# One score pass instead of two for the last head of each group, in a fused attention and feed-forward kernel

## The chip, the cores and the metric

The kernel runs on one core of one Trainium2 chip. A core has a matrix engine (TensorE, in the profile PE, its weight loads PEld), a vector engine (DVE), a scalar engine for activations (ACT), a general one (POOL) and a queue engine that issues transfers (SP). The metric is device time in microseconds. Before the change the median of three runs is 551.24 us (550.49 to 552.46).

## The reference

The input x has 2048 rows of 448. Two branches are computed from it and mixed by a gate per row. Branch A is attention with a memory, in 4 segments of 512 rows and 16 heads of 28; branch B is a feed-forward layer of width 1792.

```python
for s in range(N):                                 # N = 4 segments, L = 512 rows
    qs, ks, vs = q[:, :, s], k[:, :, s], v[:, :, s]
    logits = jnp.einsum("bhqd,bhkd->bhqk", qs, ks) * scale + mask   # causal: -1e9 above
    p = _softmax(logits, axis=-1)
    a_dot = jnp.einsum("bhqk,bhkd->bhqd", p, vs)
    ...                                            # a_mem from the memory M, z of earlier segments
    outs.append(g * a_mem + (1.0 - g) * a_dot)
    ...
o = ... @ wo
b = _silu(x @ w1) @ w2
gate = _sigmoid((x * gate_w).sum(-1, keepdims=True))
return gate * o + (1 - gate) * b
```

The weights of q and k are 200 times their usual size, so the logits are large and each row's maximum has to be taken off before the exponential.

## The kernel before

float32 values are carried as pairs of float16 halves (a high part and a remainder), so most products are three matmuls that add into one bank. The work is in three stages.

1. `project`: scales of all inputs, the projections to q, k and v, the memory of the segments. q, k and v go to buffers in device memory in the layouts that the later stages read.
2. Attention, 16 groups `t` (4 segments by 4 groups) of 4 heads, together with pass 1 of the feed-forward layer (10 of its 14 blocks of 128, for all 4 segments).
3. Pass 2 of the feed-forward layer (the other 4 blocks), the output product with `wo`, and the mix. The second products of pass 2 may not start until every group's attention is stored (`attended`). The first products of pass 2 may.

Each group reads its q and k into one buffer, `ring`. Then each head goes through two score passes:

- In `maxima`, queries lie on partitions. A 512-row segment gives four row blocks i of 128 queries with 128(i+1) keys, 1280 score columns a head. DVE adds the causal mask and takes the row maximum (line 744; for the first blocks of all four heads together, line 739, with the mask added by a matmul, line 730). The maxima are transposed, split into halves and sent through device memory into two extra rows of `ring` (`mscr`, lines 752 to 759).
- In `attention`, the scores are computed again with keys on partitions and those two extra rows, so that the maximum is already taken off (line 1328, 86 rows deep, again 1280 columns). ACT takes the exponential in three pieces (line 1333). POOL sets the parts above the diagonal to zero (lines 1336 and 1339), ACT makes the high half of all 1280 columns (line 1345) and POOL the remainder in three pieces (line 1349). Keys on partitions is the layout that the product with the values needs (line 1362): 20 matmuls a head, 10 blocks for each half.

DVE adds up the result (line 1370). After four heads the group is divided by its sums and stored (`o_scr`).

The order of all instructions on every engine is fixed when the kernel is built: `Sched` is a list scheduler with a cost for each operation. Each engine takes what can start first and, among those, what has the smallest `prio`. Head n of the 64 has `prio` 10 n, its product with the values `PVP` later, the remainder `LOP` later; the feed-forward pass spreads from `FLO` to `FHI` over the same scale. On the chip each engine then runs its list in that order, waiting on semaphores. Buffers are rings; a ring with no free buffer makes the taker wait. The score banks are the three of `BK["sc"]`. The feed-forward halves are in a ring of `NW` = 12 buffers (`ghl`).

Transfers with a transpose are there before only for the output product: `features` (line 654) turns a 128 by 896 float16 tile into seven 128 by 128 blocks, on SP's queue.

Of the kernel before, what the change touches and what calls it, by code (L numbers as in the profile page):

```python
# [19 lines left out]
NG = 4  # L20
# [10 lines left out]
NEG = -1.0e30  # L31
# [6 lines left out]
HPRIO = 26.57  # L38
# [4 lines left out]
NW = 12  # L43
# [4 lines left out]
WOT = 258.31  # L48
# [3 lines left out]
LOP = 66.17  # L52
LATE = -0.07
FIRST = 104.6
WPRIO = 91.56
MAXO = 57.4
# [3 lines left out]
MP = 23.61  # L60
VF = -52.52
VA = 12.88
VS = 2.68
NV = 8
XH0 = -44.21
NF = 4
VE = 10.92
LASTQ = 6.3
WQS = -136.22
VH = 44.78  # L70
XS0 = -76.47
VC = -7.5
OT1 = -114.26
XS = 34.75
QS = -34.17
KS1 = -32.16
SS = -9.2
# [6 lines left out]
PRICE = 235.91  # L84
PRICE2 = 67.41
SLACK2 = 0.33
PVRUNS = [((1, 0), 1)]
PVP = 79.52
FLO = 50.28
FHI = 729.09  # L90
WOP = 8.33
SZ = 16.64
SZSTEP = 1.72
XPRIO = 345.51
WBP = 34.36
# [183 lines left out]
def infini_mix(ctx: ExitStack, tc: tile.TileContext, x, wq, wk, wv, wo, beta, w1, w2, out):  # L279
# [120 lines left out]
    es = const.tile([128, NSEG + 1], F32, name="es")  # L400
    wide = const.tile([128, 2 * NSEG], F32, name="wide")
# [123 lines left out]
    def by(o, i, a, b=None, op0=OP.mult, op1=OP.mult):  # L525
        if b is None:
            nc.gpsimd.tensor_scalar(o, i, a, None, op0=op0)
        else:
            nc.gpsimd.tensor_scalar(o, i, a, b, op0=op0, op1=op1)  # L529
# [20 lines left out]
    def others(s, prio, bds, own, t_own, t_gh):  # L550

        def mem():
            z = spk[:, NSEG + s:NSEG + s + 1]
            by(z, top[:, WK:WK + 1], top[:, xi(s)], 1.0 / FIT)
            by(z, z, 1.0 / UP, op0=OP.max)
            by(bds[:, s, :, DH:], own[:, :, None], z[:GW])
            by(bds[:, s, :, :DH], own[:, :, None].to_broadcast([GW, 4, DH]), z[:GW], rv[:GW, s:s + 1])

        def go():
            by(rv[:, s:s + 1], top[:, WV:WV + 1], top[:, xi(s)], 1.0 / FIT)  # L560
            by(omgs[:, s], omg, rv[:, s:s + 1])
# [12 lines left out]
        EREADY[s] = few(5, scores, PREADY[s], SCALED[WQ], SCALED[WK], prio=prio + 0.5)  # L574
        END1.append(EREADY[s])
# [134 lines left out]
    def maxima(t, o):  # L710
# [11 lines left out]
        plan = [(0, [0, 1, 2, 3]), (1, [0, 1]), (1, [2, 3])] + [(i, [h]) for h in range(4) for i in (2, 3)]  # L722
        for q, (i, hs) in enumerate(plan):
            ps = Buf(BK["sc"])
            n = 128 * (i + 1)
            p0 = o - MAXO + 40 * q / len(plan)

            def go(i=i, hs=hs, ps=ps, n=n):
                if i == 0:
                    nc.tensor.matmul(ps.v, identb, maskb[:, None, :].to_broadcast([128, 4, 128]), start=True,  # L730
                                     stop=False, skip_group_check=True)
                for j, hh in enumerate(hs):
                    u = j * n
                    nc.tensor.matmul(ps.v[:, u:u + n], rg.v[:KS, 0, hh, i * 128:(i + 1) * 128], rg.v[:KS, 1, hh, :n],  # L734
                                     start=(i > 0), stop=(i > 0 or j == 3), skip_group_check=(i == 0))

            def red(i=i, hs=hs, ps=ps, n=n):
                if i == 0:
                    nc.vector.tensor_reduce(mx.v[:, :, 0], ps.v.rearrange("p (h n) -> p h n", h=4), axis=AX.X,
                                            op=OP.max)  # L740
                    return
                for j, hh in enumerate(hs):
                    r = ps.v[:, j * n:(j + 1) * n]
                    nc.vector.tensor_tensor_reduce(r, r, MK[:, L - n:], 1.0, NEG, OP.add, OP.max,  # L744
                                                   mx.v[:, hh, i:i + 1])
            m = pe((half(512) if i == 0 else []) + half(n, len(hs)), go, *rs, *MKS, takes=[ps], uses=[rg], prio=p0)
            reds.append(dve(len(hs) * (n + 184) if i else 512, red, m, *reds[:1], takes=[] if reds else [mx], uses=[ps, mx],
                            prio=p0))
# [3 lines left out]
        f1 = pe(half(128), lambda: nc.tensor.transpose(pt.v[:16, :128], mx.v.rearrange("p h i -> p (h i)"), ident), *reds,  # L752
                takes=[pt], uses=[mx], prio=p0)
        f3 = act(128, lambda: nc.scalar.activation(mh.v[:, 0], pt.v[:16, :128], AF.Copy, scale=1.0 / TALL), f1, takes=[mh],
                 uses=[pt], prio=p0)
        f4 = dve(128, lambda: nc.vector.scalar_tensor_tensor(mh.v[:, 1], pt.v[:16, :128], 1.0 / TALL, mh.v[:, 0],
                                                             op0=OP.mult, op1=OP.subtract), f3, uses=[pt, mh], prio=p0)
        d1 = dma(16e3, lambda: start(mscr[t].rearrange("z h i n -> (h i) z n"), mh.v), f4, uses=[mh], prio=p0)
        dm = dma(16e3, lambda: start(rg.v[KS:KS + 2, 0], mscr[t].rearrange("z h i n -> z h (i n)")), d1, uses=[rg],
# [427 lines left out]
    TH, GF, PA = (tiles(fp, n, [128, L], F32, 2) for n in ("th", "gf", "pa"))  # L1187
# [66 lines left out]
    def spare(s, p0, m):  # L1254
        th, gf, g = Buf(TH), Buf(GF), Buf(GTR)
        if s not in SP:
            fetch_spare(s, p0)
        h, e0 = SP[s]
        e1 = copy(L + 110, lambda: nc.scalar.activation(th.v, h.v, AF.Tanh, scale=wide[:, NSEG + s:NSEG + s + 1]), e0, m,
                  takes=[th], uses=[h], prio=p0)  # L1260
        e2 = dve(L, lambda: nc.vector.scalar_tensor_tensor(gf.v, th.v, 1.0, h.v, op0=OP.add, op1=OP.mult), e1,
                 port=True, takes=[gf], uses=[h, th], prio=p0)
        e3 = copy(L + 110, lambda: nc.scalar.activation(g.v[:, 0], gf.v, AF.Copy, scale=hso[:, s:s + 1]), e2, m, takes=[g],
                  uses=[gf], prio=p0)
        e4 = scaled(L, lambda e: rest(e, g.v[:, 1], gf.v, hso[:, s:s + 1], g.v[:, 0]), e3, uses=[gf, g], prio=p0)
        return g, [e3, e4]

    def part(s, tb, ps, lasts, prio):
        k = s * TB + tb
        a = Buf(PA)  # L1270
        w = act(D + 110, lambda: nc.scalar.activation(a.v[:, :D], ps.v[:, :D], AF.Copy, scale=ogs[:, k:k + 1]),
                lasts[-1][0], takes=[a], uses=[ps], prio=prio)
        PST[k] = dma(229e3, lambda: start(pscr[s][tb * 128:(tb + 1) * 128, :], a.v[:, :D]), w, uses=[a], prio=prio)
# [25 lines left out]
    cring("phl", [128, 2, 1280], F16, 3, cp)  # L1299
    cring("oraw", [128, 4, TB, DH + 1], F32, 2, cp)  # L1300
# [3 lines left out]
    t_one = [ONE[1]] + [ones_rows(i) for i in range(1, 4)]  # L1304

    def attention(t):
# [9 lines left out]
        for hh in range(4):  # L1316
            n = 4 * t + hh
            p0 = 10.0 * n
            pf, hl = Buf(C["pf"]), Buf(C["phl"])
            ex, mk = [], []  # L1320
            for b in range(3):
# [14 lines left out]
            mk.append(pool(80, lambda pf=pf: nc.gpsimd.affine_select(  # L1336
                pf.v[:, 1, 384:], pf.v[:, 1, 384:], [[1, 128]], OP.is_ge, 0.0, base=0, channel_multiplier=-1), ex[1],
                uses=[pf], prio=p0))
            mk.append(pool(204, lambda pf=pf: nc.gpsimd.affine_select(  # L1339
                pf.v[:, :, :128], pf.v[:, :, :128], [[0, 3], [1, 128]], OP.is_ge, 0.0, base=0, channel_multiplier=-1),  # L1340
                *ex, uses=[pf], prio=p0))
# [6 lines left out]
            for u, w in zip((0,) + CUTS, CUTS + (1280,)):  # L1348
                low = pool(w - u + 22, lambda hl=hl, flat=flat, u=u, w=w: nc.gpsimd.tensor_sub(  # L1349
                    hl.v[:, 1, u:w], flat()[:, u:w], hl.v[:, 0, u:w]), low, uses=[pf, hl], prio=p0 + LOP,  # L1350
                    lat=0.0 if w < 1280 else LATE)
            ps = Buf(BK["cc"])
            last = None
            for zs, ready in PVRUNS:
                def go(zs=zs, ps=ps, hl=hl, hh=hh):
# [9 lines left out]
                last = pe([m for z in zs for m in [(max(x, 0.027), y) for x, y in half((58, 29)[z], 10)]], go, dv, (hi, low)[ready], last,  # L1365
                          takes=[ps] if last is None else [], uses=[ps, hl, vg], prio=p0 + PVP)

# [3 lines left out]
            fins.append(dve(232, fin, last, *fins[:1], takes=[] if fins else [orw], uses=[ps, orw], prio=p0 + PVP))  # L1371
# [146 lines left out]
```

## Time and profile before

| | |
|---|---|
| median of 3 runs | 551.24 us |
| profiled execution, its own time | 550.28 us |
| its span (first to last instruction) | 548.5 us |
| time around the span | 1.8 us |
| PE busy | 539.2 us (98%) |
| ACT busy | 409.0 us (75%) |
| DVE busy | 401.5 us (73%) |
| POOL busy | 354.3 us (65%) |
| DMA engines, mean busy share | about 50% |

A busy time is the union of an engine's instructions; a PE that counts as busy need not be at its peak, since matmuls overlap. The profile also gives: busy time in chosen stretches of the span; the chain of work that ended last, followed back from the last instruction, with the start and the length of each piece; groups of instructions, with the busy time, the mean length of one, the idle time of the engine just before them and what ended it; the instructions in order of time; and the waits.

### The profile page before, as it was taken

The numbers are of one execution on the slowest core, as the hardware profiler recorded it, in microseconds if no ns is written. First come the engines' busy times: TensorE is split into PE (matmuls) and PEld (weight loads), VectorE is DVE, ScalarE is ACT, GpSimd is POOL, SyncE is SP. The second block draws the span as 40 slices with busy tenths as digits, with TensorE's granted clock in tenths as the row PEclk, the third lists the DMA queues.
The fourth block names the chain that finished last, engine by engine and source line by source line (L and its number), as shares of the span: only waits on it lengthen the run. The fifth ranks groups of instructions, "written<-read, shape, count | busy, mean of one in ns | idle before, by whom it ended". The sixth has DMA issues, their size and how long they took to land.

```text
span 548.5 us, 11583 instructions
## 1 busy us (share of the span) xinstructions
PE 539.2 (98%) x4044; PEld 299.7 (55%) x4044; DVE 401.5 (73%) x989; ACT 409.0 (75%) x700; POOL 354.3 (65%) x546
## 2 busy tenths in 40 slices
PE   8999999999999999999999999999999999999997
PEld 3445656556644556555565555565555555555544
DVE  5998989898668985598555788757886239754482
ACT  5978899677359978999787998889997897501140
POOL 3345374686406788899888898898998986112120
PEclk9999999999999999999999999999999999999999
DMA  8777867544467343324233234546211211689963
GB/s 300 254 238 225 243 180 219 166 148 131 140 190 189 95 129 92 103 71 120 55 112 93 70 97 115 152 121 175 56 36 36 87 54 50 238 226 233 241 177 99
DMA packets 78059, 78.94 MB, mean 144 GB/s; under 512 B 44168, under 2 KB 67720, under 8 KB 78000
## 3 DMA queue, kind: packets, MB, share of 16 engines
q1 hardware_dynamic: 77424, 77.21, 48.8%
q10 hardware_dynamic: 576, 0.99, 0.6%
q8 instruction: 32, 0.52, 0.4%
q14 instruction: 27, 0.22, 0.1%
HBM read 48.41 MB, written 26.09 MB: 136 GB/s over the span
## 4 chain that ended last, share of the span: by engine, by line
PE 74%; ACT 7%; DVE 7%; POOL 6%; DMA 3%; issue 2%; SPq 0%; DVEq 0%; ACTq 0%; POOLq 0%
PE mm L629 19%; PE mm L1232 17%; PE sc L629 8%; PE sc L1328 6%; PE sc L734 5%; PE cc L1362 5%; PE cc L1232 5%; PE cc L629 5%; ACT pf L1333 3%; DMA rawf<-in_w_dram 2%; PE sc L989 2%; POOL es L529 1%; ACT phl L1345 1%; DVE stg L931 1%; DMA raw<-in_wv_dram 1%
## 5 line engine op out<-in xcount | busy, mean ns | idle before, releaser
L1349 POOL TENSOR_TENSOR phl<-pf,phl 128x384 f16<-128x384 f32 (+1 forms) x192 | 190.4, 1011 | 22.3 <-ACT phl L1345 22.3
L1333 ACT ACTIVATE pf<-sc,lift,es 128x512 f32<-128x512 f32 (+1 forms) x192 | 127.1, 711 | 16.1 <-PE sc L1328 14.7
L744 DVE CUSTOM_DVE_ANT_0 sc<-sc,mk 128x384 f32<-128x384 f32 (+1 forms) x192 | 105.9, 570 | 31.7 <-PE sc L734 29.7
L1232 PE MATMUL mm<-wb,ghl 128*128 128x448 f16 (+2 forms) x516 | 112.0, 348 | 0.0
L629 PE MATMUL mm<-xh,wa 128*128 128x512 f16 x429 | 107.5, 379 | 0.0
L1232 PEld LDWEIGHTS <-ghl 128*128 128x128 f16 x684 | 64.0, 97 | 51.9 <-issue 0.6
L1345 ACT ACTIVATE phl<-pf 128x1280 f16<-128x1280 f32 x64 | 81.4, 1274 | 9.3 <-POOL pf L1339 8.9
L629 PEld LDWEIGHTS <-wa 128*128 128x128 f16 x572 | 53.7, 97 | 52.8 <-issue 0.2
L1328 PE MATMUL sc<-ring 86*128 86x512 f16 (+3 forms) x256 | 63.3, 300 | 0.4 <-DVE mx L744 0.3
L734 PE MATMUL sc<-ring 84*128 84x128 f16 (+3 forms) x256 | 57.8, 299 | 0.1
L1362 PEld LDWEIGHTS <-phl 128*128 128x128 f16 x1280 | 42.0, 96 | 10.6
L640 POOL TENSOR_TENSOR ol<-ol,ml 128x448 f32<-128x448 f32 x12 | 13.6, 1132 | 51.5 <-DMA ol<-o_scr 30.0
L1362 PE MATMUL cc<-vg,phl 128*128 128x29 f16 (+1 forms) x1280 | 43.6, 182 | 0.0
L629 PE MATMUL mm<-xh,wqs 128*128 128x512 f16 x176 | 42.6, 380 | 0.0
L629 PE MATMUL mm<-xh,wks 128*128 128x512 f16 x176 | 42.1, 380 | 0.0
L646 ACT ACTIVATE oh<-ol,os 128x448 f16<-128x448 f32 x16 | 10.6, 664 | 38.7 <-POOL ol L640 38.7
L1370 DVE TENSOR_REDUCE oraw<-cc 128x116 f32<-128x232 f32 x64 | 25.3, 396 | 18.3 <-PE cc L1362 17.9
L1232 PE MATMUL cc<-wb,ghl 128*128 128x448 f16 x168 | 38.4, 352 | 0.0
L1328 PEld LDWEIGHTS <-ring 86*128 86x128 f16 x256 | 24.2, 97 | 23.5 <-issue 0.9
L629 PE MATMUL cc<-xh,wa 128*128 128x512 f16 x143 | 36.7, 379 | 0.0
L629 PE MATMUL sc<-wos,oT 128*128 128x448 f16 x176 | 35.8, 353 | 0.0
L1339 POOL TENSOR_SCALAR_AFFINE_SELECT pf<-pf 128x384 f32<-128x384 f32 x64 | 33.3, 520 | 3.0 <-ACT pf L1333 2.2
(190 smaller groups left out, 937.1 us busy)
## 6 DMA issues: line engine op xcount, KB each, us to landing
rawf<-in_w_dram SPq DMA_DIRECT2D x26, 256.0 KB
rawf<-in_w_dram SPq DMA_DIRECT2D x28, 224.0 KB
v_scr<-vt SPq DMA_DIRECT2D x16, 232.0 KB
vg<-v_scr SPq DMA_DIRECT2D x16, 232.0 KB
xraw<-in_x_dram SPq DMA_DIRECT2D x14, 256.0 KB
q_scr<-stg SPq DMA_DIRECT2D x16, 224.0 KB
k_scr<-stg SPq DMA_DIRECT2D x16, 224.0 KB
ring<-q_scr SPq DMA_DIRECT2D x16, 224.0 KB
```

The costliest lines, as they stand in the source:

```text
L629: nc.tensor.matmul(ps(), *p[i], start=(i == 0), stop=(i == n - 1))
L640: d = pool(530, lambda: nc.gpsimd.tensor_add(b.v, b.v, m.v), d, e, uses=[b, m], **k)
L734: nc.tensor.matmul(ps.v[:, u:u + n], rg.v[:KS, 0, hh, i * 128:(i + 1) * 128], rg.v[:KS, 1, hh, :n], start=(i > 0), stop=(i > 0 or j == 3), ...
L744: nc.vector.tensor_tensor_reduce(r, r, MK[:, L - n:], 1.0, NEG, OP.add, OP.max, mx.v[:, hh, i:i + 1])
L1232: nc.tensor.matmul(ps.v[:, lo:hi], g.v[:, y, sl], w.v[:, z, lo:hi], start=(j == 0 and i == 0), stop=(j == len(fs) - 1 and i == 2))
L1328: nc.tensor.matmul(ps.v[:, e:e + w], rg.v[:KK, 1, hh, j * 128:(j + 1) * 128], rg.v[:KK, 0, hh, j * 128:], start=True, stop=True)
L1333: ex.append(sact(e, lambda b=b, ps=ps, pf=pf, e=e: nc.scalar.activation(pf.v[:, b, :e], ps.v[:, :e], AF.Exp, bias=lift, scale=es[:, s:s + ...
L1339: mk.append(pool(204, lambda pf=pf: nc.gpsimd.affine_select(pf.v[:, :, :128], pf.v[:, :, :128], [[0, 3], [1, 128]], OP.is_ge, 0.0, base=0, ...
L1345: hi = copy(1280, lambda hl=hl, flat=flat: nc.scalar.activation(hl.v[:, 0], flat(), AF.Copy), *mk, takes=[hl], uses=[pf], prio=p0 + 2)
L1349: low = pool(w - u + 22, lambda hl=hl, flat=flat, u=u, w=w: nc.gpsimd.tensor_sub(hl.v[:, 1, u:w], flat()[:, u:w], hl.v[:, 0, u:w]), low, u ...
L1362: nc.tensor.matmul(p[:, i, :2 - z], hl.v[:, z, u:u + 128], vg.v[:, j, hh, :2 - z], start=(z == zs[0] and i == 0), stop=(z == zs[-1] and j ...
L1370: nc.vector.tensor_reduce(orw.v[:, hh], p, axis=AX.X, op=OP.add)
```

## The change

The last head of each group (`TURNED` = 1), in all groups but the first, gets a single score pass.

- `maxima` leaves this head out. Its mask matmul has 384 columns instead of 512, and the rows sent through `mscr` are those of three heads.
- A new function `scores` computes the head's scores with queries on partitions, in three banks: block 3 (512 columns), blocks 2 and 0 (384 and 128), block 1 (256). DVE adds the mask and takes the row maximum of each block. ACT makes minus the scaled maximum plus a constant, one ACTIVATE on 128x1 for each block, and then the exponential of each block with that as its bias, four instead of three.
- The two selections on POOL are not needed, as masked scores become zero in the exponential; for that `NEG` is -1e38.
- The halves are made as before, into `phl`, but with queries on partitions. Two transfers with a transpose on SP, one for each half, ten 128 by 128 blocks each, write `pht`, from which the product with the values reads.
- The head's scores have a `prio` that is `TLEAD` = 41.9 earlier than its place; its product comes at `TVP` instead of `PVP`.
- Two more small instructions on POOL for each segment make `nes`, the negative of the scale.
- For space: `ghl` has 11 buffers instead of 12, the `gf` ring goes (the spare block works in place in `th`), `pa` is 448 wide instead of 512.
- Some forty constants of the scheduler (`prio` offsets and prices) have other values, so the order of instructions differs in all stages.

```diff
-NW = 12
+NW = 11
+TURNED = 1
+TLEAD = 41.9
+TLOW = -26.78
+TVP = 12.29
+NTURN = 1
...
-FLO = 50.28
-FHI = 729.09
+FLO = 52.62
+FHI = 689.43
...
+            by(es[:, s:s + 1], es[:, s:s + 1], 2.0 ** -100, op0=OP.max)
+            by(nes[:, s:s + 1], es[:, s:s + 1], -1.0)
...
-        plan = [(0, [0, 1, 2, 3]), (1, [0, 1]), (1, [2, 3])] + [(i, [h]) for h in range(4) for i in (2, 3)]
+        nh = 4 - TURNED if t else 4
+        plan = [(0, range(nh)), (1, range(min(nh, 2)))] + ([(1, range(2, nh))] if nh > 2 else [])
+        plan += [(i, [h]) for h in range(nh) for i in (2, 3)]
...
+    cring("pht", [128, 2, 1280], F16, NTURN, cp)
+    cring("nb", [128, 2, TB], F32, 2 * TURNED, cp)
...
+    def scores(t, hh, rg, rs, pf, prio):
+        s, nb, ex = t // NG, Buf(C["nb"]), []
+        for rows in ((3,), (2, 0), (1,)):
+            ps = Buf(BK["sc"])
...
+            def go(at=at, ps=ps):
+                for i, lo, hi in at:
+                    nc.tensor.matmul(ps.v[:, lo:hi], rg.v[:KS, 0, hh, i * 128:(i + 1) * 128], rg.v[:KS, 1, hh, :hi - lo],
+                                     start=True, stop=True)
+            def red(at=at, ps=ps):
+                for i, lo, hi in at:
+                    r = ps.v[:, lo:hi]
+                    nc.vector.tensor_tensor_reduce(r, r, MK[:, L - (hi - lo):], 1.0, NEG, OP.add, OP.max, nb.v[:, 0, i:i + 1])
+            def drop(at=at):
+                for i, lo, hi in at:
+                    nc.scalar.activation(nb.v[:, 1, i:i + 1], nb.v[:, 0, i:i + 1], AF.Identity, bias=lift, scale=nes[:, s:s + 1])
+            def exps(at=at, ps=ps):
+                for i, lo, hi in at:
+                    nc.scalar.activation(pf.v.rearrange("p b n -> p (b n)")[:, 64 * i * (i + 1):64 * (i + 1) * (i + 2)], ps.v[:, lo:hi],
+                                         AF.Exp, bias=nb.v[:, 1, i:i + 1], scale=es[:, s:s + 1])
...
+            turned = t > 0 and hh >= 4 - TURNED
...
+            if turned:
+                pq, low0 = p0 + TVP, TLOW
+                p0 -= TLEAD
+                mk = scores(t, hh, rg, rs, pf, p0)
-            for b in range(3):
+            for b in range(0 if turned else 3):
...
-            mk.append(pool(80, lambda pf=pf: nc.gpsimd.affine_select(
+            if not turned:
+                mk.append(pool(80, lambda pf=pf: nc.gpsimd.affine_select(
...
+            if turned:
+                pr = Buf(C["pht"])
+                land = [sch.add("SP", TUS * 10 / 7, lambda z=z, pr=pr, hl=hl: nc.sync.dma_start_transpose(
+                    pr.v[:, z].rearrange("p (b q) -> p b q", b=10), hl.v[:, z]), [d], takes=[] if z else [pr], uses=[hl, pr],
+                    prio=p0, lat=TLAT) for z, d in enumerate((hi, low))]
...
-                                u = off[j] + 128 * (i - j)
+                                u = 64 * i * (i + 1) + 128 * j if turned else off[j] + 128 * (i - j)
```

More of the change, by code (lines that the diff above doesn't have):

```diff
@@ L51 @@
 SLACK = -0.5
[L52 to L56, printed above, removed]
+LOP = 63.28
+LATE = -0.1
+FIRST = 166.08
+WPRIO = 65.13
+MAXO = 60.98
 FULL = 0.111
@@ L59 @@
 RB = "cc"
[L60 to L63, printed above, removed]
+MP = 25.49
+VF = -55.25
+VA = 12.69
+VS = 3.39
 NV = 8
-XH0 = -44.21
+XH0 = -53.53
 NF = 4
[L67 to L71, printed above, removed]
-VC = -7.5
[L73 to L77, printed above, removed]
+VE = 0.78
+LASTQ = 6.05
+WQS = -123.0
+VH = 51.92
+XS0 = -53.05
+VC = -7.5
+OT1 = -150.13
+XS = 41.57
+QS = -34.91
+KS1 = -30.59
+SS = -11.48
 def VP(o, k):
     return o + VA + VS * k if o or k > VF else -1.0 + 0.1 * k
-PRICE = 235.91
-PRICE2 = 67.41
-SLACK2 = 0.33
+PRICE = 218.62
+PRICE2 = 41.61
+SLACK2 = 0.34
 PVRUNS = [((1, 0), 1)]
-PVP = 79.52
-FLO = 50.28
-FHI = 729.09
[L91 to L95, printed above, removed]
+PVP = 65.99
+FLO = 52.62
+FHI = 689.43
+WOP = 107.76
+SZ = 16.55
+SZSTEP = 0.11
+XPRIO = 368.0
+WBP = 35.98
 XLEAD = 146.82
@@ L729, in go @@
                 if i == 0:
-                    nc.tensor.matmul(ps.v, identb, maskb[:, None, :].to_broadcast([128, 4, 128]), start=True,
+                    nc.tensor.matmul(ps.v[:, :nh * n], identb, maskb[:, None, :].to_broadcast([128, nh, 128]), start=True,
                                      stop=False, skip_group_check=True)
@@ L1186, in infini_mix @@
     RG.n = len(rgt)
-    TH, GF, PA = (tiles(fp, n, [128, L], F32, 2) for n in ("th", "gf", "pa"))
+    TH, PA = tiles(fp, "th", [128, L], F32, 2), tiles(fp, "pa", [128, D], F32, 2)
     WBR = tiles(fp, "wb", [128, 2, D], F16, len(PASSES[0]))
@@ L1364, in go @@
                                                  skip_group_check=True)
-                last = pe([m for z in zs for m in [(max(x, 0.027), y) for x, y in half((58, 29)[z], 10)]], go, dv, (hi, low)[ready], last,
-                          takes=[ps] if last is None else [], uses=[ps, hl, vg], prio=p0 + PVP)
+                last = pe([m for z in zs for m in [(max(x, 0.027), y) for x, y in half((58, 29)[z], 10)]], go, dv, *(land + fins[:1] if turned else (land[ready],)),
+                          last, takes=[ps] if last is None else [], uses=[ps, pr, vg], prio=pq)
             def fin(hh=hh, ps=ps):
@@ L1370, in fin @@
                 nc.vector.tensor_reduce(orw.v[:, hh], p, axis=AX.X, op=OP.add)
-            fins.append(dve(232, fin, last, *fins[:1], takes=[] if fins else [orw], uses=[ps, orw], prio=p0 + PVP))
+            fins.append(dve(232, fin, last, *fins[:1], takes=[] if fins else [orw], uses=[ps, orw], prio=pq))
         rl, ob = Buf(C["rl"]), Buf(C["ob"])
```

74 lines of the change are left out of this document (43 added, 31 removed).

## The prediction

> **What bounds the kernel now.** I read the busy table first, then the busy time by stretches, then the chain that ended last.
>
> ```profile
> span 548.5 us, 11583 instructions
> PE 539.2 (98%) x4044; PEld 299.7 (55%) x4044; DVE 401.5 (73%) x989; ACT 409.0 (75%) x700; POOL 354.3 (65%) x546
> ```
>
> The averages hide the stage that changes. Attention runs from about 165 us (first exponential at 167.8) and its last exponential starts at 451.3; the last store of attended rows is issued at 464.2:
>
> ```profile
> core 0: us, PE busy (x) PEld busy (x) DVE busy (x) ACT busy (x) POOL busy (x), PEclk, DMA share, GB/s
> 165.00:185.00 20.00, 19.54 (x147) 10.11 (x145) 17.59 (x51) 19.17 (x32) 14.61 (x19) 1.00 0.58 154
> 225.00:245.00 20.00, 19.88 (x195) 11.29 (x194) 15.57 (x43) 19.51 (x32) 17.98 (x26) 1.00 0.26 69
> 165.00:445.00 280.00, 279.02 (x2584) 160.23 (x2582) 200.19 (x575) 249.57 (x370) 245.15 (x339) 1.00 0.35 98
> 445.00:548.00 103.00, 99.81 (x592) 51.38 (x590) 62.20 (x103) 37.16 (x60) 29.77 (x32) 1.00 0.63 173
> ...
> L1333 ACT ACTIVATE pf<-sc,lift,es x192: 542/768/845, 167.8 to 451.3; 128x512 f32<-128x512 f32 x128, 128x256 f32<-128x256 f32 x64
> L364 SPq DMA_DIRECT2D o_scr<-ob x16: 370/396/1000, 195.2 to 464.2; - x16
> ```
>
> In those 280 us PE lacks 1 us of being full, ACT lacks 30.4 us and POOL 34.9 us. So two engines stand close behind PE, and the best that ACT reaches in any 20 us is 19.51 (97.5%) and 19.17 (96%). The granted clock is 1.00 throughout.
>
> ```profile
> 37.76 3.32 POOL es L529
> 112.61 3.51 POOL es L529
> 154.00 7.12 PE mm L629 x33
> 443.23 1.25 ACT pf L1333 x2
> 468.04 6.81 PE mm L1232 x36
> 540.43 2.08 PE sc L629 x11
> ```
>
> In the chain the pace of PE can be read: 36 matmuls of 448 columns in 6.81 us and 33 of 512 in 7.12 us, both 0.42 ns a column. The mean durations of single matmuls (below, 217 to 380 ns) contain the pipeline's latency and are not what one costs. At 443 the chain is on ACT, and from 468.04 PE runs the second feed-forward product of pass 2, which may not start before all attention is stored. Between them PE is fed by first products of pass 2. So the end of attention, not only PE's sum of work, decides when the tail of 80 us begins.
>
> **PE: what goes.** Fifteen heads (one in each group but the first) lose their second score pass.
>
> ```profile
> L1328 PE MATMUL sc<-ring 86*128 86x512 f16 x64 | 24.3, 380 | 0.1
> L1328 PE MATMUL sc<-ring 86*128 86x384 f16 x63 | 20.6, 327 | 0.3 <-DVE mx L744 0.3
> L1328 PE MATMUL sc<-ring 86*128 86x256 f16 x63 | 17.2, 274 | 0.0
> L1328 PE MATMUL sc<-ring 86*128 86x128 f16 x63 | 13.7, 217 | 0.0
> L730 PE MATMUL sc<-maskb,identb 128*128 128x512 bf16 x14 | 5.3, 379 | 0.5 <-ACT pf L1333 0.4
> ```
>
> A head has 512+384+256+128 = 1280 columns, at 0.42 ns 0.54 us; 15 heads 8.1 us. The mask matmul shrinks by 128 columns in 15 groups, 0.8 us. The scores of the turned head itself replace those of the first pass, column for column, and the 20 products with the values stay. PE: -8.9 us; the stage would need 271 us of it.
>
> **ACT: what comes.** The turned head needs its bias per row, so a small ACTIVATE on 128x1 for each of four row blocks, then four exponentials instead of three.
>
> ```profile
> L1333 ACT ACTIVATE pf<-sc,lift,es 128x512 f32<-128x512 f32 x126 | 94.3, 779 | 14.8 <-PE sc L1328 13.5 <-POOL phl L1349 0.9
> L1333 ACT ACTIVATE pf<-sc,lift,es 128x256 f32<-128x256 f32 x62 | 35.4, 571 | 1.3 <-PE sc L1328 1.2
> L1209 ACT ACTIVATE th<-mm,ths 128x512 f32<-128x512 f32 x27 | 18.6, 690 | 1.6 <-PE mm L629 1.5
> L1213 ACT ACTIVATE ghl<-mm 128x512 f16<-128x512 f32 x27 | 16.1, 599 | 0.5 <-DVE mm L1211 0.4
> ...
> L1011 ACT ACTIVATE gate<-sc,tqk 128x1 f32<-128x1 f32 x12 | 3.1, 261 | 0.9 <-DVE vt L1013 0.9
> ...
> 230.83 1.93 ACT L1333 ACTIVATE pf<-sc,lift,es 128x512 f32<-128x512 f32 x3
> 232.60 0.65 ACT L1213 ACTIVATE ghl<-mm 128x512 f16<-128x512 f32 x1
> 233.08 0.25 ACT L754 ACTIVATE mhl<-sc 16x128 f16<-16x128 f32 x1
> 233.24 0.66 ACT L1209 ACTIVATE th<-cc,ths 128x512 f32<-128x512 f32 x1
> ```
>
> At one tile size, no pointer operand takes 599 ns, one (scale) 690, two (scale and bias) 779: about 90 ns each. Queued instructions overlap: three exponentials take 232.60 - 230.83 = 1.77 us of the queue, and the 128-column copy at 233.08 takes 0.16. A column costs (779-571)/256 = 0.81 ns. Four exponentials on the same 1280 columns are one more start with two pointers: 0.16 - 128x0.81 ns + 2x0.09 = 0.24 us. A small ACTIVATE has the same fixed part, so 0.24 us if it overlaps its neighbour, and 0.261 + 0.09 = 0.35 us alone. Each exponential reads what the small one before it has just written, on the same engine; no row of this trace shows ACT waiting for itself, so I keep both ends. Per turned head +0.24 + 4 x (0.24 to 0.35) = 1.2 to 1.64 us, for 15 heads 18 to 25 us. I take 23, nearer the upper end, because three of the four groups of small ones have to finish before what follows. ACT: 249.6 + 23 = 272.6 us of work, in a stage for which PE now wants 271. The copy into halves (L1345) is unchanged. The small ACTIVATE also adds a wait: it stands in ACT's queue until DVE has the row maximum, and behind it stand tanh, copies and exponentials of other heads, for which PE's next products and POOL wait; that is where a full ACT reaches PE.
>
> The Trainium skill's page "ScalarE: Activation LUTs", section "What ACT_TABLE_LOAD costs", gives 186 ns plus 0.833 ns a column, about 93 ns more for each pointer operand and about 93 ns of overlap between neighbours. The trace agrees with the pointers (91 and 89 ns). By the Trainium skill's figures a small ACTIVATE would be 0.28 us overlapped, and the sum over 15 heads an estimated 20 us.
>
> **DVE and POOL.**
>
> ```profile
> L744 DVE CUSTOM_DVE_ANT_0 sc<-sc,mk 128x512 f32<-128x512 f32 x60 | 42.3, 704 | 16.7 <-PE sc L734 16.0
> L744 DVE CUSTOM_DVE_ANT_0 sc<-sc,mk 128x256 f32<-128x256 f32 x60 | 25.0, 437 | 1.0
> L744 DVE DVE_READ_ACCUMULATOR2_ANT mx<- 128x1 f32 x180 | 25.4, 141 | 0.0
> L1339 POOL TENSOR_SCALAR_AFFINE_SELECT pf<-pf 128x384 f32<-128x384 f32 x62 | 32.3, 520 | 2.9 <-ACT pf L1333 2.2 <-ACT mhl L754 0.2
> L1336 POOL TENSOR_SCALAR_AFFINE_SELECT pf<-pf 128x128 f32<-128x128 f32 x62 | 18.2, 293 | 7.2 <-ACT pf L1333 6.3 <-PE cc L629 0.7
> L527 POOL TENSOR_SCALAR spk<-spk 128x1 f32<-128x1 f32 x6 | 2.2, 374 | 0.5
> ```
>
> DVE gets one reduction of 128 columns with its read: 437 - 128 x (704-437)/256 = 304, plus 141, less 128 columns (133 ns) of the common one: +0.31 us a head, 4.7 us in all, on an engine with 80 us free. POOL loses both selections, 0.81 us a head, 12.2 us: it goes to 233 and is the engine that gains most. Two more POOL instructions per segment in front of the scores' readiness (0.37 us each) stand behind `es`, which is on the chain at 37.76 and 112.61: 0 to 1.5 us. PE is nearly full there too (chain pieces of PE on both sides), so I take 0.
>
> **The transposing transfers.** 30 are added on SP's queue.
>
> ```profile
> L654 SPq DMA_TRANSPOSE oT<-oh x16: 1222/1230/2007, 348.9 to 533.4; - x16
> ...
> SPq L364 <- PE sc L734: 37.5, 15, 7.5
> ```
>
> Issuing one of seven blocks holds SP 1.23 us; ten blocks 1.76 us, 53 us in the stage. The last of the old ones is issued at 533.4 and its product starts at 540.43, so landing takes at most 7.0 us and at least the 1.23. Behind a transfer that waits on SP stand the next group's ring loads, the stores of finished rows and the weights; SP already waits, 2.5 us a time, for buffers that PE reads. The diff asks for the turned head's scores 41.9 units early, four heads ahead at 10 a head, so some 17 us (280 us for 64 heads is 4.4 a head) cover two issues (3.5) and 7.0 of landing. I price it at 0; without that cover, issue and landing less the 0.81 us of selections, 4 to 10 us once, at the last group, since the others have a next group to work on. DMA share is 0.35 in the stage, so bandwidth is free. One buffer fewer for the feed-forward halves (12 to 11) can cost at most one first product of cover before 468, 7.12/3 = 2.4 us; I take 0, since three units of three products fit.
>
> **The sum.** PE would allow 280 - 8.9 = 271 us. ACT has 272.6 us of work there, and in-order queues that depend on each other don't fill: at 96 to 97.5%, its best stretches, the stage takes 280 to 284 us, taken 282.5 (96.5%). That is +2.5 us on the profiled execution, 548.5 + 1.8 around it = 550.28, so 552.8. The median of the runs, 551.24, is 1.0 above it: 553.8, said as 554. With 18 to 25 us on ACT and 95 to 98% of filling the stage takes 273 to 289 us: 544.5 to 560.5 on the median. The cause would be that the work saved on PE comes back as a longer ACT queue.
>
> **Rivals.**
>
> *PE's gain arrives.* ACT's tail is empty (37 of 103 us), and what the feed-forward pass asks of ACT can slip behind attention. If it does, ACT is not the bound and the stage follows PE: -8.9 us, 542.3; with some waits 542 to 547. For it: POOL, the second neighbour, is relieved by 12 us. Against it: ACT's 30.4 us of idle time is nearly all spent. It decides if ACT's addition stays under about 15 us or a like amount is moved. 30%.
>
> *A bank is held too long.* In the turned head a score bank goes PE, DVE, ACT, ACT before it is free (0.38 + 0.70 + 0.14 + 0.35 + 0.78 = 2.35 us for 512 columns, as long as both old visits together, but in one piece), there are three, and ACT is full. PE issues in order, so a score matmul without a bank stops the feed-forward work behind it. There are 45 such passes; from 8.9/45 = 0.2 us of PE waiting in each the saving is gone. At 0.4 us it is 18 - 8.9 = +9 us, 560; at 0.5, 565. For it: DVE and ACT both wait in line today; against it: PE hardly ever waits now. 12%.
>
> *PE is not the bound.* Then 8.9 us less of it gives nothing, and 23 us more fit into ACT's idle 30: 551, no change. The 55% of weight loading speaks for it. Against it: at 0.42 ns a column, PE has no gap between the chain's pieces. The Trainium skill's "Perfetto Trace Analysis", section "Identifying the Most-Contended Engine", says to judge TensorE by weight-loading share and use of its peak, not by matmul busy time; by the first, PE has room, and the trace's column pace speaks against it. 8%.
>
> **How the numbers follow.** A difference under 0.3%, 1.7 us, can't be told from none. The forecast has 50%: 38 slower, 6 within, 6 faster. The first rival gives 28 faster, 2 within; the second 12 slower; the third 3 within, 1 faster, 4 slower. Together faster 0.35, same 0.11, slower 0.54. The likeliest case alone spans 548 to 560; the range for 8 in 10 leaves out the best of the first rival and the worst of the second: 544 to 562.
>
> **What would show it.** Right: ACT busy over 96% between 165 and the end of attention, PE with several us of waits for ACT in that stretch (now 1 us in all), POOL under 86%, the second pass 15 heads shorter, the last attended store at 464 or later. Wrong: PE still full there and that store before 458, or ACT's small instructions under 0.2 us each. If PE waits for score banks while ACT has gaps, the second rival holds; waits of PE for transposed tiles would show that my cover fails.

## The result, and the profile after

The changed kernel takes 558.3 us (557.28 to 559.56, 4 runs) against 551.07 for the kernel before: a ratio of 1.0129 (1.010 to 1.0157), 7.2 us slower. The forecast was slower, 554.0, in a range of 544 to 562. The direction and the cause hold; the rise was more than twice what the sum gave.

The page of the profile after, its span, two busy rows and the chain's shares by engine:

```profile
span 557.8 us, 11621 instructions
PE 540.5 (97%) x3984; PEld 296.4 (53%) x3984; DVE 400.1 (72%) x1021; ACT 428.0 (77%) x771; POOL 344.2 (62%) x528
...
PEclk9999999999999999999999999999799999999999
...
PE 57%; ACT 26%; POOL 6%; DVE 4%; issue 4%; DMA 2%; SPq 0%; DVEq 0%; ACTq 0%
```

ACT has 19 us more of busy time than before (428.0 against 409.0) and holds 26% of the chain that ended last. The same page of the kernel before gives

```profile
PE 74%; ACT 7%; DVE 7%; POOL 6%; DMA 3%; issue 2%; SPq 0%; DVEq 0%; ACTq 0%; POOLq 0%
```

Busy time by stretches, after; the columns are those of the prediction:

```profile
225.00:245.00 20.00, 18.96 (x170) 10.32 (x168) 15.60 (x44) 19.75 (x34) 15.31 (x21) 1.00 0.44 104
385.00:405.00 20.00, 17.75 (x148) 9.18 (x147) 14.16 (x41) 17.84 (x31) 16.43 (x23) 0.83 0.67 134
165.00:445.00 280.00, 271.36 (x2437) 152.12 (x2436) 198.81 (x598) 261.96 (x432) 231.07 (x306) 0.99 0.53 128
165.00:465.00 300.00, 290.50 (x2631) 162.76 (x2630) 206.53 (x612) 281.24 (x462) 248.68 (x328) 0.99 0.52 125
```

PE now lacks 8.6 us in the 280 where it lacked 1.0. In the stretch at 225 us ACT is full and PE is not. POOL has fallen from 245 to 231 us. The attended rows are stored 8 us later (472.3 against 464.2), and the score passes, which waited for almost nothing before, now wait for ACT (groups of instructions, the first two rows before, the last two after; the idle time before them and what ended it are on the right):

```profile
L734 PE MATMUL sc<-ring 84*128 84x128 f16 (+3 forms) x256 | 57.8, 299 | 0.1
L1328 PE MATMUL sc<-ring 86*128 86x512 f16 (+3 forms) x256 | 63.3, 300 | 0.4 <-DVE mx L744 0.3
...
L744 PE MATMUL sc<-ring 84*128 84x384 f16 (+2 forms) x196 | 47.6, 301 | 3.9 <-ACT pf L1345 2.0 <-ACT pf L1385 1.7
L1380 PE MATMUL sc<-ring 86*128 86x512 f16 x196 | 45.8, 302 | 4.8 <-ACT pf L1385 3.1 <-ACT pf L1345 0.7 <-DVE mx L754 0.5
```

The transfers of the attended rows, with their first and last start:

```profile
L369 SPq DMA_DIRECT2D o_scr<-ob x16: 370/406/655, 202.9 to 472.3; - x16
```

Idle time understates it, because a matmul that stood alone is drawn with its whole latency: a score matmul lasts 301 ns by these rows, while its 320 columns (the mean of the four widths) take 0.13 us at 0.42 ns a column. So I also take, between 165 and 480 us, the time from one matmul's start to the next, less 0.42 ns a column (at least 27 ns), and add up what is over 0.1 us. This is called PE's lost time below: 2.5 us before, 19.3 us after. Some 15 of the 19.3 us stand ahead of the matmuls of the two score passes, and nearly as much, 14.6, is ended by an exponential that frees a bank. About 2.4 of the rest are matmuls that run at half clock (see the last section).

One turned head on ACT, after, in order of time:

```profile
225.42 0.37 ACT L1341 ACTIVATE nb<-nb,lift,nes 128x1 f32<-128x1 f32 x1
225.82 0.78 ACT L1345 ACTIVATE pf<-sc,nb,es 128x512 f32<-128x512 f32 x1
226.50 0.65 ACT L1341 ACTIVATE nb<-nb,lift,nes 128x1 f32<-128x1 f32 x2
227.06 1.01 ACT L1345 ACTIVATE pf<-sc,nb,es 128x384 f32<-128x384 f32 x2
227.95 0.39 ACT L1341 ACTIVATE nb<-nb,lift,nes 128x1 f32<-128x1 f32 x1
228.37 0.56 ACT L1345 ACTIVATE pf<-sc,nb,es 128x256 f32<-128x256 f32 x1
228.97 1.27 ACT L1398 ACTIVATE phl<-pf 128x1280 f16<-128x1280 f32 x1
```

All small instructions as one group (ns, shortest, median and longest):

```profile
L1341 ACT ACTIVATE nb<-nb,lift,nes x60: 371/376/387, 183.3 to 446.5; 128x1 f32<-128x1 f32 x60
```

From 225.42 to 228.97 the head holds ACT 3.55 us, where a plain head holds it 1.77. Where one small instruction stands directly ahead of the exponential that reads it (blocks 3 and 1), the exponential starts 0.40 to 0.42 us after it, and 0.37 to 0.39 of that is its length: they don't overlap. Where two stand together (blocks 2 and 0), they do overlap: they start 0.28 us apart, and the first exponential starts 0.28 us after the second of them, since it reads the first. By this head, 15 x 1.78 = 26.7 us of ACT's queue go into 60 columns' worth of results.

### The profile page after: what moved, and what is told of

It reads as the page before. It is cut to its first block, busy times and chain, and to the rows that moved or that the text cites. A ratio compares the mean times of both kernels' runs of the same rounds, so it can differ in the third digit from the quotient of the medians.

```text
span 557.8 us, 11621 instructions
## 1 busy us (share of the span) xinstructions
PE 540.5 (97%) x3984; PEld 296.4 (53%) x3984; DVE 400.1 (72%) x1021; ACT 428.0 (77%) x771; POOL 344.2 (62%) x528
## 4 chain that ended last, share of the span: by engine, by line
PE 57%; ACT 26%; POOL 6%; DVE 4%; issue 4%; DMA 2%; SPq 0%; DVEq 0%; ACTq 0%
PE mm L637 14%; PE mm L1243 13%; PE sc L637 9%; ACT phl L1398 5%; ACT pf L1385 5%; PE cc L1243 5%; PE cc L637 4%; ACT pf L1345 4%; PE sc L744 3%; PE sc L1380 3%; PE cc L1421 3%; ACT th L1220 2%; ACT nb L1341 2%; POOL phl L1402 2%; DMA xraw<-in_x_dram 1%
## 5 line engine op out<-in xcount | busy, mean ns | idle before, releaser
L1402 POOL TENSOR_TENSOR phl<-pf,phl 128x384 f16<-128x384 f32 (+1 forms) x192 | 188.0, 1002 | 40.5 <-ACT phl L1398 40.5
L754 DVE CUSTOM_DVE_ANT_0 sc<-sc,mk 128x256 f32<-128x256 f32 (+2 forms) x147 | 81.2, 568 | 30.5 <-PE sc L744 25.9
L1385 ACT ACTIVATE pf<-sc,lift,es 128x512 f32<-128x512 f32 x147 | 96.8, 719 | 6.2 <-PE sc L1380 6.0
L744 PE MATMUL sc<-ring 84*128 84x384 f16 (+2 forms) x196 | 47.6, 301 | 3.9 <-ACT pf L1345 2.0
L1380 PE MATMUL sc<-ring 86*128 86x512 f16 x196 | 45.8, 302 | 4.8 <-ACT pf L1385 3.1
L1421 PEld LDWEIGHTS <-phl 128*128 128x128 f16 x980 | 32.4, 96 | 11.5 <-issue 4.2
L1220 ACT ACTIVATE th<-mm,ths 128x512 f32<-128x512 f32 x39 | 27.0, 696 | 12.2 <-PE mm L637 10.6
L1345 ACT ACTIVATE pf<-sc,nb,es 128x512 f32<-128x512 f32 (+3 forms) x60 | 35.1, 611 | 1.4
L1226 DVE SCALAR_TENSOR_TENSOR ghl<-mm,ghl 128x512 f16<-128x512 f32 x39 | 26.6, 685 | 12.1 <-ACT ghl L1224 12.0
L1421 PE MATMUL cc<-vg,phl 128*128 128x29 f16 (+1 forms) x980 | 33.9, 183 | 0.3 <-POOL phl L1402 0.3
```

The costliest lines, as they stand in the source:

```text
L1220: e1 = sact(L, lambda ps=ps, th=th: nc.scalar.activation(th.v, ps.v, AF.Tanh, scale=ths[:, s:s + 1]), m, takes=[th], uses=[ps], prio=p0)
L1226: e4 = dve(L, lambda ps=ps, g=g: nc.vector.scalar_tensor_tensor(g.v[:, 1], ps.v, DOWN, g.v[:, 0], op0=OP.mult, op1=OP.subtract), e3, uses= ...
L1345: nc.scalar.activation(pf.v.rearrange("p b n -> p (b n)")[:, 64 * i * (i + 1):64 * (i + 1) * (i + 2)], ps.v[:, lo:hi], AF.Exp, bias=nb.v[: ...
L1380: nc.tensor.matmul(ps.v[:, e:e + w], rg.v[:KK, 1, hh, j * 128:(j + 1) * 128], rg.v[:KK, 0, hh, j * 128:], start=True, stop=True)
L1385: ex.append(sact(e, lambda b=b, ps=ps, pf=pf, e=e: nc.scalar.activation(pf.v[:, b, :e], ps.v[:, :e], AF.Exp, bias=lift, scale=es[:, s:s + ...
L1421: nc.tensor.matmul(p[:, i, :2 - z], hl.v[:, z, u:u + 128], vg.v[:, j, hh, :2 - z], start=(z == zs[0] and i == 0), stop=(z == zs[-1] and j ...
```

## The experiments

Theory 1: ACT's queue is the bound. Rival 1: a score bank is held too long. Rival 2: the transposing transfers. Rival 3: the order that comes with the new constants. Times are medians; each ratio is to the kernel before, run on the same chip.

**e1: the small bias instructions on DVE, order kept.**

```diff
-nc.scalar.activation(nb.v[:, 1, i:i + 1], nb.v[:, 0, i:i + 1], AF.Identity, bias=lift, scale=nes[:, s:s + 1])
+nc.vector.tensor_scalar(nb.v[:, 1, i:i + 1], nb.v[:, 0, i:i + 1], nes[:, s:s + 1], LIFT, op0=OP.mult, op1=OP.add)
```

> The changed kernel with the order of every engine kept, but the 60 small instructions that make the bias (128x1) run on DVE instead of ACT. Theory 1 (ACT's queue is the bound of attention): a turned head holds ACT 3.55 us in the changed kernel's order of instructions against 1.77 before, and the small ones with the waits behind them are about 1.3 us of it, 20 us over 15 heads; so the time falls from 558 to 546 to 552. Rival 1 (score banks held too long): the chain of steps in a bank stays, only one step gets shorter by some 0.2 us: 555 to 558. Rival 2 (the transposing transfers) and rival 3 (the other order of instructions): no change, 557 to 559.

Measured: 552.27 us, ratio 1.0022 (1.0006 to 1.0037), at the edge of what theory 1 gave (546 to 552) and well below the rivals. Moving 60 instructions on 128 elements gives back 6.0 of the 7.2 us. PE's lost time falls to 13.5 us, and the last attended store is at 465.8. ACT's busy time is that of the kernel before again. But ACT now waits for DVE (e1: the busy row of the page, then ACT's waits with total, times, longest):

```profile
PE 537.3 (98%) x3984; PEld 295.7 (54%) x3984; DVE 404.3 (73%) x1081; ACT 410.0 (75%) x711; POOL 345.3 (63%) x528
```

```profile
ACT pf L1345 <- DVE nb L1341: 14.6, 20, 1.7
```

Of the 18 us of busy time taken off ACT, 14.6 came back as waits in its queue. What is left to explain is why PE, with 8.9 us less to do, doesn't bring the kernel below 551.

**e2: no turned head, all other edits.**

```diff
-TURNED = 1
+TURNED = 0
```

> The changed kernel with no turned head (TURNED = 0), but with all its other edits: the new constants and so the new order, 11 buffers for the feed-forward halves, the smaller rings, two more small POOL instructions per segment. Theory 1: ACT has its old work back, so 549 to 553. Rival 3 (the order or the 11 buffers cost the time): 555 to 560.

Measured: 571.55 us, ratio 1.0364 (1.0349 to 1.0379). Nobody expected it: with the kernel's old arithmetic, the new constants, the 11 buffers and the smaller rings together cost 20 us. An order made for one set of instructions doesn't carry over to another, so this run cannot price the order in the changed kernel, and rival 3 is not excluded by it. Part of the loss is another thing (busy time by stretches, e2; the clock is the number after POOL):

```profile
215.30:218.70 3.40, 1.93 (x26) 1.03 (x26) 2.43 (x10) 2.60 (x4) 3.35 (x4) 1.00 0.46 127
218.70:242.60 23.90, 21.50 (x172) 11.32 (x172) 14.88 (x45) 19.10 (x26) 22.96 (x33) 0.50 0.30 80
```

After 3.4 us in which PE was busy a little over half the time, the granted clock was 0.50 for 23.9 us, which is up to 12 us of PE.

**e3: plain transfers in place of transposing ones.**

```diff
-nc.sync.dma_start_transpose(pr.v[:, z].rearrange("p (b q) -> p b q", b=10), hl.v[:, z])
+nc.sync.dma_start(pr.v[:, z], hl.v[:, z])
```

> The changed kernel with the 30 transposing transfers replaced by plain transfers of the same bytes between the same tiles; this leaves out the turn of the probabilities, so the turned heads' products are taken of probabilities that are not turned. All orders stay. Theory 1: the transfers are not the bound, 556 to 558.5. Rival 2 (small packets, 0.53 instead of 0.35 of the transfer engines, SP held 1.38 us each): 549 to 554.

Measured: 559.04 us, ratio 1.0136 (1.0118 to 1.0154), no faster. Rival 2 is out. The transposes were dear in themselves: SP is held three times as long for one (transfers into `pht`, after, then e3), and the transfer engines' share is 0.53 against 0.44 in the stage. It was all hidden.

```profile
L1408 SPq DMA_TRANSPOSE pht<-phl x30: 1332/1382/2038, 188.7 to 452.9; - x30
```

```profile
L369 SPq DMA_DIRECT2D pht<-phl x30: 465/471/581, 188.9 to 452.8; - x30
```

**e4: the kernel before with ACT's extra work alone.**

```diff
+for k in range((1, 2, 1)[b] if more else 0):      # more: last head of 15 groups
+    nc.scalar.activation(spent[:, k:k + 1], lift, AF.Identity, bias=lift, scale=es[:, s:s + 1])
 nc.scalar.activation(pf.v[:, b, :e], ps.v[:, :e], AF.Exp, ...)   # b = 1: two pieces, 384 and 128
```

> The kernel before with ACT's extra work alone: in the last head of 15 groups four small ACTIVATEs of 128x1 with two pointer operands, whose result nobody reads, and the second exponential cut into 384 and 128 columns. Order, banks and transfers are those of before. Without the waits of one ACTIVATE for another this is 15 x (4 x 0.28 + 0.24) = 20 us more on ACT, which has 30 us idle. Theory 1: 554 to 560, though nothing is saved on PE. Rivals 1, 2 and 3: ACT has room, 551 to 552.5.

Measured: 559.22 us, ratio 1.0137 (1.0123 to 1.0150): 7.9 us slower, as much as the change. ACT's busy time rose by 18 us (427.0), so each us of ACT cost 0.44 us. The busy row of the page, that of the stage, and PE's longest wait, e4:

```profile
PE 543.2 (97%) x4044; PEld 300.4 (54%) x4044; DVE 402.8 (72%) x989; ACT 427.0 (77%) x775; POOL 354.8 (64%) x546
...
165.00:445.00 280.00, 275.46 (x2513) 156.50 (x2512) 200.38 (x572) 259.32 (x430) 238.05 (x329) 1.00 0.35 96
```

```profile
PE sc L735 <- ACT pf L1340: 2.6, 7, 0.7
```

Here no bank passes through more engines, nothing is transposed and the order is the old one. Theory 1 stands on this run and e1. ACT's 30 us of idle time in the kernel before did not take the 18 us up.

**e5 and e6: ACT relieved elsewhere.** The high halves of pass 1 are made by DVE, in e1 (e5) and in the kernel before (e6), orders kept.

```diff
-nc.scalar.activation(g.v[:, 0], ps.v, AF.Copy, scale=DOWN)
+nc.vector.tensor_scalar(g.v[:, 0], ps.v, DOWN, None, op0=OP.mult)      # pass 1 only
```

> The kernel of e1 (small bias instructions on DVE) with ACT relieved once more at a place that has nothing to do with the turned heads: in pass 1 of the feed-forward layer the high half (a copy of 512 columns, 0.48 us of ACT's queue) is made by DVE. Orders stay. That takes some 17 us off ACT in the attention stage and puts some 20 on DVE, which has 75 free there. Theory 1 (ACT's queue): PE's saving of 8.9 us now arrives, 543 to 548 after 552.3. Rival 1 (the steps of a turned head hold a score bank too long, whoever is loaded): 551 to 554.

> The kernel before with the same relief (high halves of pass 1 on DVE), as the control for e5: ACT goes from 250 to some 233 us in the 280 us of attention, where PE already lacks only 1 us of being full. Theory 1: PE is the bound there, so 550 to 551.5, no change. If ACT's lateness costs the kernel before something as well, 545 to 549, and then e5 says less about the turned heads.

Measured: e5 553.5 us, 1.0042 (1.0026 to 1.0058); e6 553.94, 1.0045 (1.0033 to 1.0058). Theory 1 expected 543 to 548 of e5 and missed. PE's lost time in e5 is 13.5 us as in e1, but less of it is now ended by ACT (6.7 us against 8.8) and more by a row maximum on DVE (4.8 against 2.4; e5, PE's longest wait, then two of the four stretches in which first products run):

```profile
PE sc L1381 <- DVE mx L754: 2.9, 5, 0.8
```

```profile
225.00:245.00 20.00, 19.32 (x169) 10.29 (x168) 18.93 (x57) 15.87 (x24) 15.54 (x21) 1.00 0.45 111
325.00:345.00 20.00, 19.07 (x177) 10.81 (x175) 18.74 (x59) 16.68 (x25) 17.84 (x24) 1.00 0.72 184
```

DVE had 77 us free over the stage (203 of 280 in e1), but in these stretches it is 94% full with the added work. So an engine's slack over a stage isn't slack where it is needed. e6 fits it in the old kernel, where the expected no change was a loss of 2.7 us: in two of these stretches (245 and 325 us) DVE is busy 19.3 and 19.6 of 20 us.

**e7 and e8: the turned head's bank freed early.** e7 is e1 with the buffer of the exponentials taken at the row maximum, which moves the order a little; e8 has that order, and DVE writes the masked scores to that buffer instead of the bank.

```diff
-nc.vector.tensor_tensor_reduce(r, r, MK[...], ...)                # r: the bank
+nc.vector.tensor_tensor_reduce(pf_part, r, MK[...], ...)          # pf_part: the block's part of pf; the exponential reads it
```

> The kernel of e1, planned as if a turned head took its buffer for the exponentials already at the row maximum. Only the order changes by it (some 3% of PE's rows stand elsewhere). It is the control for e8: 551 to 555 by all theories.

> As e7, in the same order, but DVE writes the masked scores of the turned head into the buffer of the exponentials instead of back into the score bank, and ACT takes the exponential from there. So a turned head's bank is free after DVE (0.38 + 0.84 us), without ACT. ACT pays some 0.04 us more for each of 60 exponentials, 2.4 us. Rival 1 (banks held too long): 4 to 9 us below e7. Theory 1 (ACT's queue, at every head): within 2 us of e7.

Measured: 551.69 (1.001, 0.9991 to 1.003) and 551.65 us (1.0004, 0.9992 to 1.0016). No difference: that the turned head holds its bank through four steps costs nothing that can be seen. ACT is busy 2.3 us more in e8 (412.3 against 410.0), which at 0.44 could hide 1 us, not the 4 to 9 that rival 1 gave. Rival 1 in the form of the prediction is out.

**e9 and e10: any free bank, orders kept.** A pass takes the bank, of all eight, that has been free longest.

```diff
-p = self.places[self.at]
+p = places[min(free, key=lambda i: last[i].free_at if last[i] else 0.0)]     # places: of all three rings
```

> The kernel of e1 with every engine's order kept, instruction for instruction, but a score pass takes whichever of the eight banks has been free longest, where before it had the three score banks in turn (and the feed-forward products and the products with the values likewise). If what is left of the loss is that PE comes to a score matmul before one of three banks is free (in e1 and in e5 PE's waits stand ahead of lines 744 and 1380, and are ended by DVE or ACT, whichever is late): 544 to 549, and those waits shrink. If it is ACT's or DVE's lateness itself, the next product waits for the same late instruction a little later: 550.5 to 553.

> The kernel before with the same free choice of banks and its own order: the control for e9. PE lacks 1 us of being full in attention, so 549.5 to 551.5 by all theories.

Measured: e9 549.7 us, 0.9966 (0.9953 to 0.9979); e10 549.98, 0.9975 (0.9965 to 0.9985). e9 is faster than both kernels, but e10 is so by as much: the free choice is worth 2.6 us in e1 and 1.4 in the kernel before, and the turned head on top of it is worth nothing that can be told from noise. PE's lost time in e9 is still 10.7 us. The time lies between the two expectations: banks matter a little, and PE still waits, at other places.

**e11: the kernel before with PE's saving alone.**

```diff
+if less:                                       # last head of 15 groups: 64 columns in each bank, j = b
+    nc.tensor.matmul(ps.v[:, :64], rg.v[:KK, 1, hh, j * 128:(j + 1) * 128], rg.v[:KK, 0, hh, j * 128:j * 128 + 64], ...)
+    return
...                                             # the exponential reads the 64 columns again and again
```

> The other half of the change alone: the kernel before, in its own order, with PE's work cut and ACT's, DVE's and POOL's kept. In the last head of 15 groups the second score pass computes 64 columns in each of its three banks instead of 512, 512 and 256, and the exponential reads those 64 again and again; this leaves out most scores of these heads. PE has 15 x 1088 columns less, at 0.42 ns 6.8 us. If PE bounds attention, as its 279 of 280 us say: 543.5 to 546. If PE, ACT, DVE and POOL are each full in some stretches, so that one of the others holds the place as soon as PE is shorter: 548 to 551.

Measured: 547.46 us, 0.9935 (0.9921 to 0.9948): 3.6 us for 6.8 us of PE, 0.53 us for each, between the two expectations. The stage of this run:

```profile
165.00:445.00 280.00, 278.38 (x2597) 159.25 (x2596) 202.55 (x579) 251.75 (x375) 247.23 (x341) 1.00 0.36 101
```

PE still counts as nearly full although it has less to do. It looks as if PE bound about half of the stage's time and something else the other half; only the price is measured.

**e12: a new order.** e9's free banks, the small instructions on DVE, and an order searched with mended costs.

```diff
-sact(e, ...)                          # exponential of a plain head
+act(e + 211, ...)                     # two pointer operands
-act(150 * len(at), drop, ...)
+dve(100 * len(at), drop, ...)
...                                    # the cost of a turned head's exponentials, 37 constants of the order
```

> A version meant to be faster than both: the changed kernel with the small bias instructions on DVE, a free choice of banks as in e9, and a new order of all engines, searched with the scheduler's costs mended by what the traces show: an exponential with two pointer operands costs ACT 0.09 us more than it assumed, the further block of a turned head 0.235 us, and the small instructions cost DVE 0.17 us and ACT nothing. If what is left of PE's saving was lost because the order of instructions counts on an ACT that is faster than it is, so that PE comes to the score passes too early: 543 to 548. If it is lost because several engines are full in the same stretches whatever the order: 549 to 552. Searched orders can also be worse on the chip than by their costs: up to 556.

Measured: 551.24 us, 0.9995 (0.9982 to 1.0009). The waits in ACT's queue shrank and those of PE too (lost time 8.7 us, clock 1.00 throughout), but the time is that of the kernel before (waits in e12, ACT's and PE's):

```profile
ACT pf L1370 <- DVE nb L1366: 3.6, 7, 0.7
...
PE mm L1009 <- DVE ph L992: 3.0, 3, 1.7
```

The second row is in the projections, ahead of the attention. PE is busy 158.8 of the first 165 us, against 160.4 before, and the first exponential starts at 171.4 us instead of 167.8: this order lost time there, and may have won some of it back later. That a better order could bring the saving out is therefore neither shown nor excluded.

## Why the prediction was right, and where it was off

**PE's saving.** That 60 matmuls go was right (4044 to 3984). That it lets the stage fall to 271 us was not: e11 prices a us of PE in this stage of the kernel before at 0.53 us, and at that price 8.9 us are worth 4.7.

**ACT's addition.** The terms were about right. A small instruction takes 0.376 us, a little above the bound of 0.35; it holds the queue 0.28 us where the next instruction doesn't read it and 0.40 us or more where it does. Busy time grew by 19 us and the queue's time by some 26.7, on both sides of the 23 taken. e1 and e4 show that this is the cause, e4 without any other part of the change.

**The filling of ACT.** This step failed. I let ACT reach 96.5% over the stage, as in its best 20 us, and got +2.5 us. It reached 281.24 of 300, 93.7%, until the attended rows were near their end, and these came 8.1 us later. In the prediction's own terms, 272.6 us of work took 280 + 8.1 = 288.1 us, a filling of 94.6%, just under the 95 to 98% that it allowed; its range still held the result, since it also took up to 25 us of work. The named sign, ACT over 96%, did not show. A part of the reason can be seen: the load comes in four stretches, where the first products of the feed-forward pass bring tanh and halves to ACT and DVE, and between them ACT has room and PE has none. Before, ACT was busy 19.51 of the 20 us from 225 us, and between two such stretches (before)

```profile
265.00:285.00 20.00, 20.00 (x187) 11.90 (x186) 10.66 (x35) 15.93 (x22) 18.00 (x26) 1.00 0.33 94
```

Work put on ACT in a full stretch finds no idle time there, and that of another stretch can't take it. But the four stretches (165 to 186, 221 to 262, 294 to 334 and 373 to 418 us, 147 of the 315) hold 12.0 of the 19.3 us of PE's lost time after, and 6.0 of 10.2 in e4; the rest arises between them, so the stretches are not the whole reason, and what the rest is stays open.

The better sum prices both loads by the runs on the kernel before: 19 x 0.44 - 8.9 x 0.53 = +3.6 us, and of the measured 7.2 some 3.6 are left. Busy time leaves out the 0.1 us and more that ACT stands still or doesn't overlap where an exponential reads the small instruction just ahead. In e4 nobody reads the small ones, they start 0.28 us apart, and with the cut exponentials they take 60 x 0.278 + 15 x 0.24 = 20.2 us of the queue, 0.39 us of time for each. By queue time the sum is 26.7 x 0.39 - 4.7 = +5.7 us, and 1.5 are left. Both are estimates, and no run decides between them.

**The clock.** The prediction counted with 1.00. After a stretch with PE little more than half busy, it was 0.50 for 6.8 us of the profiled execution, 3.4 us of PE, and this execution took 559.56; the one with the highest mean clock, 0.999, took 557.28. If all of that difference is the clock, it is 2.3 us of the slowest run and about 1 us of the median; four runs can't show it, since those of the kernel before spread over 2 us as well. The last 0.5 to 2.6 us, by one price or the other, stay open; the order, which differs from that of e4 and e11, is a candidate, and e2 shows only that an order with its rings can cost far more than that.

**POOL, DVE, transfers.** POOL fell to 83% (under 86 was said). DVE's 4.7 us don't show: it is busy 198.8 us of the stage, against 200.2 before. One transpose holds SP 1.38 us and not the 1.76 taken, no matmul waits for a transposed tile, and e3 shows that the cover held.

**The rivals.** PE's gain arriving: no, since ACT's addition was not under 15 us. It didn't arrive in e1 either, where ACT's busy time was back; there the turned head's steps made ACT wait 14.6 us, but that these waits are the whole reason isn't shown, as e12 has few of them and is no faster. The held bank: PE's waits are at score banks, as this rival said, but neither freeing them early (e8) nor a free choice (e9) brings the saving; the reading left is that a bank is late because the engine that frees it is late. PE not the bound: half true, by e11. The Trainium skill's rule in "Perfetto Trace Analysis", section "Identifying the Most-Contended Engine", warns that matmul busy time doesn't tell how much room PE has. The trace agrees as far as a PE shown at 100% had some; its weight-loading share of 55% doesn't say how much, and e11 prices it.

## What to carry to other kernels

When several engines are each about 90% full over a stage, price a change by what a us on each engine moves, in the stretches where it lands, and not by the idle time of the stage: here 0.44 for ACT and 0.53 for PE, so 19 us of ACT outweighed 9 us of matmuls. An instruction on one column is not a small one (0.376 us here for one result per row), and one that the next instruction reads is paid in full (0.40 us of the queue, against 0.28 where another stands between). A wait moved from one full engine to another (e5) is not removed: look who ends the wait now.

## What the runs showed of the hardware

PE's granted clock fell to 0.50 without PE having been idle for long: it was busy 1.77 of 3.40 us ahead of the drop in the changed kernel, 1.92 in e1 and 1.93 in e2, in pieces. It then stayed low for 6.8, 3.4 and 23.9 us. The stretch ahead of the drop, after and e1:

```profile
391.80:395.20 3.40, 1.77 (x26) 1.10 (x26) 3.34 (x10) 3.37 (x6) 3.32 (x4) 1.00 0.15 29
```

```profile
388.40:391.80 3.40, 1.92 (x33) 1.12 (x30) 3.40 (x10) 3.40 (x7) 3.32 (x4) 1.00 0.50 92
391.80:395.20 3.40, 3.40 (x23) 1.63 (x20) 2.08 (x6) 3.40 (x7) 3.21 (x8) 0.50 1.14 164
```

The busy share alone doesn't decide it. In e3 the drop followed 3.4 us with PE busy for 2.30; in e6 and e12 the clock stayed at 1.00 through windows with 1.70 and 1.71, and after them (e3, e6, e12):

```profile
391.40:394.80 3.40, 2.30 (x29) 1.19 (x27) 3.09 (x10) 3.33 (x7) 3.23 (x5) 1.00 0.00 0
...
48.20:51.60 3.40, 1.70 (x11) 0.86 (x10) 2.81 (x7) 3.32 (x8) 0.87 (x3) 1.00 0.33 99
...
104.90:108.30 3.40, 1.71 (x12) 1.06 (x11) 2.14 (x4) 3.05 (x9) 2.08 (x6) 1.00 0.00 0
```

The Trainium skill's "TensorE: Matmul & The Clock Gate", Part 1, has the clock halved after an idle window of about 3.4 us. The halving agrees; here it followed windows with PE busy for 52 to 68%, and not every window with 50%. Small waits of PE, added up, can thus cost a second time, through the clock; what share of work keeps it up stays open.
